# Adjacent-head pairs, stacked AV outputs and 64x64 diagonal transposes in a fused attention and bilinear-FFN kernel

## The chip, the cores and the metric

One Trainium2 chip, one of its cores. The metric is device time in microseconds (us) of one execution; lower is better. Each job below ran its kernels one after the other on the same chip, with runs of the kernel before between them. The record calls a run slow when it is over 1.5% above the fastest of the same kernel. The others are fast, and only they are compared: a ratio is the mean time of one kernel's fast runs over that of the other's fast runs of the same rounds. The medians and ranges quoted beside it are over all runs. They take in the slow ones, so the ratio is not quite that of the medians.

## The reference, cut to what matters

```python
# batch 8, heads 8, sequence 576, head 64; 8 global tokens; FFN 4608 tokens, 512 -> 1536 -> 512
mask = np.abs(pos[:, None] - pos[None, :]) <= 32
mask = mask | is_global[:, None] | is_global[None, :]
scores = np.where(mask, scale * np.matmul(q, k.transpose(0, 1, 3, 2)), -1e9)
attn = softmax(scores)                       # rows of global tokens see all keys
x = np.matmul(attn, v)                       # then heads side by side: (4608, 512)
out = ((x @ w_a) * (x @ w_b)) @ w_out
```

## The kernel before: the parts that the change and the argument touch

The kernel records every operation in a graph, and a list scheduler with fixed constants puts each engine's instructions into one static order. Attention of one batch is interleaved with the FFN of earlier ones. A "unit" is two heads over half of the sequence.

```python
# prologue: 14 warm-up matmuls of 512 columns, bound to PSUM bank 7
return e.matmul(psum[:, 7, :], onz[:, 0:2, :], HT[:, 0, 0:512], start=True, stop=True)

# q, k of the first two batches: one head's 64 rows at a time, transposed on PE,
# and the global tokens' columns by a chain of 9 one-hot matmuls (zeros and single ones, to pick columns)
for j in range(j0, j1):
    i = e.transpose(flat[:, 64 * j : 64 * j + 64], src[:, j, :], ident[xs, xs])
for j in range(9):
    i = e.matmul(gl, src[:, j, :], oh9[xs, j, x, :], start=(j == 0), stop=(j == 8), ...)

# rows of the global tokens: 8 plain transfers per tensor, the token from a register
src = (q, k, v)[t][:, :, bass.ds(regs[id(e), "tok"][gi], 1), :].rearrange("b h o d -> b (h o) d")
return e.dma_start((gathq, gathk, gathv)[t][gi::8, :, :], src)

# AV of a unit: V and ones side by side, 128 columns, one PSUM bank for each head
i = e.matmul(ops[:, hh, 0:OC]..., vb[sl][0:kk, c, hh, x : x + 2, :], eb[es][0:kk, hh, ...]...)
# then log, exp(-) and multiply on 64 partitions x 576; scatter of the 8 global tokens:
eng = ("DVE", "ACT")[gi % 2]
# ... cut ...
```

The softmax here doesn't subtract the row's maximum and nothing guards it: scores larger than these inputs give would overflow.

## Time and profile before

| | before |
|---|---|
| median (first job) | 395.75 us, 4 runs of 395.44 to 398.04 |
| PE busy, share of the span | 94% |
| first FFN matmul | 34.4 us |
| from there to the third 512-token FFN group | 92.5 us, PE idle 10.8 of them |
| from there to the end | 265.5 us |

The third group's start is taken here as the start of the ACT copy that follows its first matmuls (126.9 us). The three stretches add up to the span, so a difference between two kernels can be put into one of them. The profile's lines and how to read them are in the prediction below. Timeline columns: start, length, engine, source line, operation, times; in brackets the idle time before and what ended it.

```profile
123.10 0.56 DVE L610 COPY xT<-xg 128x4 bf16 x4
123.56 0.52 ACT L609 ACTIVATE xT<-xg 128x4 bf16 x4
...
124.14 0.61 PE L940 MATMUL psum<-xT,wb 128*128 128x512 bf16 x1 [1.28 <-ACT xT L609]
```

The scatter of eight tokens is shared by DVE and ACT, four copies each, and PE's FFN waits 1.28 us for its end.

### The profile page before, as it was taken

What the parts mean: (1) busy time and instruction counts of PE and PEld (TensorE: products, weight loads), DVE (VectorE), ACT (ScalarE), POOL (GpSimd) and SP (SyncE); (2) the same over time, 40 slices, a digit from 0 to 9 for tenths busy, and PEclk for the clock granted to TensorE, in tenths of its full rate; (3) what the DMA queues carried; (4) which work ended last, traced back from release to release, by engine and by line L of the source; (5) the groups of instructions that cost most, each with busy time, mean ns of one, the idle gap of its engine ahead of it and who ended that gap; (6) DMA issues with size and microseconds to landing.
All of it is one profiled execution on the core that took longest, in us unless ns stands there. A gap on an engine that the chain in (4) does not pass through costs nothing.

```text
span 392.4 us, 6734 instructions
## 1 busy us (share of the span) xinstructions
PE 368.4 (94%) x2532; PEld 190.1 (48%) x2532; DVE 242.9 (62%) x478; ACT 242.8 (62%) x417; POOL 97.6 (25%) x163
## 2 busy tenths in 40 slices
PE   3898998978985999999999999999999999999996
PEld 0567886434442444444444444444444444444442
DVE  6875688577877675867786677666767632222220
ACT  1576788676886676677776777776767633323322
POOL 5992095033813410601430430201000000000000
PEclk9569999899995999999999999999999999999999
DMA  6999999689897087966597636300000000100012
GB/s 217 255 282 184 201 243 173 153 226 275 195 270 173 14 118 185 250 171 155 186 229 161 189 90 162 90 28 27 29 28 28 27 27 28 53 28 27 34 48 107
DMA packets 122735, 52.66 MB, mean 134 GB/s; under 512 B 105143, under 2 KB 112879, under 8 KB 122703
## 3 DMA queue, kind: packets, MB, share of 16 engines
q1 hardware_dynamic: 113871, 47.24, 47.3%
q0 software_dynamic: 8352, 4.92, 8.6%
q8 instruction: 20, 0.33, 0.3%
q10 hardware_dynamic: 480, 0.07, 0.1%
q14 instruction: 12, 0.10, 0.1%
HBM read 39.97 MB, written 9.44 MB: 126 GB/s over the span
## 4 chain that ended last, share of the span: by engine, by line
PE 89%; DVE 7%; issue 1%; ACT 1%; POOL 0%; DVEq 0%; ACTq 0%
PE psum L940 48%; PE psum L977 24%; PE psum L839 7%; PE psum L757 5%; PE psum L792 2%; PE psum L685 2%; PE psum L752 1%; DVE xT L857 1%; DVE eb L830 1%; DVE HT L953 1%; PE psum L688 1%; PE psum L586 1%; DVE xT L610 1%; DVE kT L488 0%; DVE gsb L868 0%
## 5 line engine op out<-in xcount | busy, mean ns | idle before, releaser
L940 PE MATMUL psum<-xT,wb 128*128 128x512 bf16 (+2 forms) x480 | 127.7, 360 | 3.9 <-DVE xT L610 2.7
L940 PE MATMUL psum<-xT,wa 128*128 128x512 bf16 (+2 forms) x480 | 129.7, 360 | 0.0
L953 DVE TENSOR_TENSOR HT<-psum,bc 128x512 bf16<-128x512 f32 (+1 forms) x114 | 75.5, 663 | 81.4 <-PE psum L940 75.2
L977 PE MATMUL psum<-wo,HT 128*128 128x512 bf16 x432 | 123.8, 384 | 0.0
L948 ACT ACTIVATE bc<-psum 128x512 f32<-128x512 f32 (+1 forms) x114 | 65.5, 574 | 58.5 <-PE psum L940 57.3
L857 DVE TENSOR_TENSOR xT<-psum,rec 64x576 bf16<-64x576 f32 x56 | 64.3, 1148 | 12.9 <-ACT rec L854 12.0
L827 ACT ACTIVATE eb<-psum 128x960 bf16<-128x960 f32 x56 | 54.2, 969 | 22.1 <-PE psum L757 21.1
L940 PEld LDWEIGHTS psum<-xT,wb 128*128 128x128 bf16 x480 | 44.7, 98 | 46.7 <-ACT eb L827 2.9
L940 PEld LDWEIGHTS psum<-xT,wa 128*128 128x128 bf16 x480 | 45.5, 98 | 43.0 <-issue 0.9
L977 PEld LDWEIGHTS psum<-wo,HT 128*128 128x128 bf16 x432 | 40.0, 98 | 44.9 <-issue 3.8
L830 DVE TENSOR_TENSOR eb<-eb,mask 128x960 bf16<-128x960 bf16 x56 | 40.2, 718 | 20.8 <-ACT eb L827 20.1
L848 ACT ACTIVATE rec<-psum 64x576 f32<-64x576 f32 x56 | 36.0, 644 | 15.6 <-PE psum L839 15.0
L854 ACT ACTIVATE rec<-rec 64x576 f32<-64x576 f32 x56 | 37.9, 677 | 0.9
L984 ACT ACTIVATE ost<-psum 128x512 f32<-128x512 f32 x36 | 21.5, 597 | 26.9 <-PE psum L977 26.7
L839 PE MATMUL psum<-eb,vb 125*128 125x170 bf16 (+1 forms) x336 | 34.8, 244 | 2.6 <-DVE eb L830 2.6
L839 PEld LDWEIGHTS psum<-eb,vb 125*128 125x128 bf16 x336 | 29.2, 102 | 15.6 <-DVE eb L830 4.2
L757 PE MATMUL psum<-qT,kT 64*128 64x210 bf16 (+4 forms) x384 | 25.6, 241 | 5.3 <-DVE xT L857 4.6
L610 POOL CAST vb<-vs 128x640 bf16<-128x640 f32 (+2 forms) x26 | 17.6, 703 | 42.8 <-PE psum L839 42.8
L757 PEld LDWEIGHTS psum<-qT,kT 64*128 64x128 bf16 x384 | 11.8, 95 | 31.6 <-issue 13.4
L735 POOL COPY qT<-qgT 128x128 bf16<-128x128 bf16 x12 | 3.8, 322 | 89.2 <-PE psum L757 88.2
L637 POOL CAST kb<-ks 128x640 bf16<-128x640 f32 x24 | 17.9, 786 | 1.0 <-DMA ks<-in_k_dram 1.0
L850 DVE TENSOR_REDUCE gst<-psum 128x16 f32<-128x64 f32 x56 | 12.3, 219 | 8.2 <-ACT rec L848 7.5
(110 smaller groups left out, 232.0 us busy)
## 6 DMA issues: line engine op xcount, KB each, us to landing
vs<-in_v_dram SPq DMA_DIRECT2D x39, 256.0 KB, 3.9
out_dram<-ost SPq DMA_DIRECT2D x36, 256.0 KB, 2.0
qf<-in_q_dram SPq DMA_DIRECT2D x7, 1152.0 KB, 7.9
ks<-in_k_dram SPq DMA_DIRECT2D x30, 256.0 KB, 3.7
wb<-in_moe_w_b_dram POOLq DMA_DIRECT2D x6, 256.0 KB, 14.3
wa<-in_moe_w_a_dram POOLq DMA_DIRECT2D x6, 256.0 KB, 15.8
wo<-in_moe_w_out_dram POOLq DMA_DIRECT2D x6, 256.0 KB, 8.1
ks<-in_k_dram SPq DMA_DIRECT2D x2, 576.0 KB, 8.2
```

Of the source, the lines that this page charges most:

```text
L610: return e.tensor_copy(dst, src)
L757: i = e.matmul(psum[:, ob + hh, s0 : s0 + 10 * w].rearrange("p (j w) -> p j w", j=10), kT[rs][rw, 2 * c + x, :], qT[rs][rw, :, 64 * x + pa ...
L827: G.add("ACT", act_time(2 * SC), lambda e: e.activation(eb[es][:, :, :], sps[:, :, 0:SC], AF.Exp, scale=0.125), X=skeys, W=[("eb", es)], p ...
L830: G.add("DVE", dve_time(2 * SC, 2) + 0.06, lambda e: e.tensor_tensor(eb[es][:, :, :], eb[es][:, :, :], mask[:, r, :].unsqueeze(1).broadcas ...
L839: i = e.matmul(ops[:, hh, 0:OC].rearrange("p (j w) -> p j w", j=10)[:, :, pa - 32 * r : pb - 32 * r], vb[sl][0:kk, c, hh, x : x + 2, :], e ...
L848: G.add("ACT", act_time(576), lambda e: e.activation(rec[es][ro, :, :], ops[so, :, 0:288], AF.Ln), R=okeys, W=[("rec", es)], prio=prio + 1.2)
L854: G.add("ACT", act_time(576, False), lambda e: e.activation(rec[es][ro, :, :], rec[es][ro, :, :], AF.Exp, scale=-1.0), X=[("rec", es)], pr ...
L857: G.add("DVE", 1.12, lambda e: e.tensor_tensor(xT[ro, 2 * h : 2 * h + 2, t0 : t0 + 288].rearrange("p m (w j) -> p m w j", j=9), ops[ro, :, ...
L940: i = e.matmul(psum[:, bn, n * (f - fc) : n * (f - fc) + n], w[:, kc, 128 * f : 128 * f + 128], xT[:, kc, cols], start=(kc == 0), stop=(kc ...
L948: G.add("ACT", act_time(n * nf), lambda e: e.activation(bc[bi][:, 0 : n * nf], psum[:, bk, 0 : n * nf], AF.Copy), X=[("bank", bk)], W=[("b ...
L953: G.add("DVE", dve_time(n * nf), lambda e: e.tensor_tensor(HT[:, fc : fc + nf, hcol], psum[:, ak, 0 : n * nf].rearrange("p (f n) -> p f n" ...
L977: i = e.matmul(psum[:, ok, :], HT[:, fc, 512 * hs + 128 * tt : 512 * hs + 128 * tt + 128], wo[:, fc, :], start=(fc == 0), stop=(fc == NFC ...
```

## The change

Its intent: two neighbouring heads share a PSUM tile, V's product in one bank and the sums in another, so that log, exponential and multiply work on all 128 partitions; q and k are loaded on 128 partitions and transposed by diagonal 64x64 tiles; small warm-up matmuls fill PE's gaps until bank 7 is used. Inside the same diff: indirect gathers on POOL replace the register transfers, the scatter moves to ACT (batches 0, 1) and POOL (2 to 7), and all schedule constants are new.

```diff
 # transposes and one-hots, now twice as many, each on a 64x64 tile
-for j in range(j0, j1):
-    i = e.transpose(flat[:, 64 * j : 64 * j + 64], src[:, j, :], ident[xs, xs])
+for j in range(j0, j1):
+    for y, ys in halves:
+        i = e.transpose(flat[ys, 64 * j : 64 * j + 64], src[ys, j, :], ident[ys, ys])
 # ... one-hot chains likewise ...
 # AV
-i = e.matmul(ops[:, hh, 0:OC]..., vb[sl][0:kk, c, hh, x : x + 2, :], eb...)
+for n in range(2):
+    for x in range(2):
+        lh = ones[0:kk, 0:D] if n else vb[sl][0:kk, c, 2 * m + x, :]
+        i = e.matmul(acc[64 * x : 64 * x + 64, n, :]..., lh, eb[es][0:kk, x, ...]...)
 # global rows
-return e.dma_start((gathq, gathk, gathv)[t][gi::8, :, :], src)          # 8 per tensor
+e.indirect_dma_start(grow[t][:, D * n : D * n + D], None, src,
+                     bass.IndirectOffsetOnAxis(gidx[:, 0:1]..., 0), ...)  # POOL, 4 per tensor
 # scatter of global tokens
-eng = ("DVE", "ACT")[gi % 2]
+rk = ("regs", "ACT" if b == 1 else "POOL")
 # warm-up: up to 150 matmuls of 256 columns, where PE has nothing else
-for n in range(14): G.add("PE", 0.43, fn, ..., span=(4.0 + 0.45 * n, 12.0))
+for n in range(NFILL): G.add("PE", 0.15, fn, ..., span=(1.5, FILL), lat=0.0)
 # ... loads, casts, more than 20 constants: cut ...
```

## The prediction

> **What bounds the kernel now.** I read the page's busy table first, then the slices, then the busy time by stretch, then who waited for whom on PE, then single stretches of the timeline.
>
> ```profile
> PE 368.4 (94%) x2532; PEld 190.1 (48%) x2532; DVE 242.9 (62%) x478; ACT 242.8 (62%) x417; POOL 97.6 (25%) x163
> ...
> PE   3898998978985999999999999999999999999996
> ...
> PEclk9569999899995999999999999999999999999999
> ```
>
> PE is the bound: 94% busy, the others 62% or less. So the end is the sum of PE's work, its idle time and what it loses at a lower granted clock. The slices put idle and lost clock into the first third; from slice 14 on PE is full.
>
> ```profile
> 10.80:18.25 7.45, 7.40 (x113) 4.76 (x113) 6.16 (x14) 4.17 (x13) 7.45 (x14) 0.50 1.08 219
> ...
> 34.40:66.50 32.10, 32.10 (x423) 26.55 (x421) 23.18 (x59) 24.80 (x56) 17.69 (x25) 1.00 1.22 210
> 66.50:74.00 7.50, 5.37 (x34) 2.47 (x33) 5.68 (x13) 4.91 (x10) 0.61 (x1) 0.77 1.09 214
> 74.00:86.00 12.00, 11.48 (x78) 5.35 (x75) 7.21 (x13) 8.02 (x12) 1.14 (x4) 1.00 0.52 133
> 86.00:115.20 29.20, 26.52 (x180) 13.04 (x181) 23.56 (x38) 22.70 (x38) 14.16 (x20) 1.00 0.99 247
> 115.20:128.50 13.30, 7.81 (x46) 3.93 (x45) 8.89 (x20) 8.70 (x16) 3.96 (x7) 0.62 0.72 186
> 128.50:315.00 186.50, 185.50 (x1162) 89.38 (x1162) 131.65 (x229) 134.24 (x210) 35.19 (x54) 1.00 0.46 114
> ```
>
> Columns: stretch, its length, busy us of PE, weight load, DVE, ACT, POOL, granted clock, DMA share, GB/s. From 34.4 to 66.5 and after 128.5 PE is full at clock 1.00; only less PE work can help there. What can be won lies elsewhere: a late start (first transposes at 10.8 us), 15.3 us at half clock, and 66.5 to 128.5, where PE is busy 51.2 us of 62.0 (10.8 idle) and loses about 1.7 us (7.5 x 0.23) and 5.1 us (13.3 x 0.38) to the clock.
>
> ```profile
> PE psum L685 <- DVE kb L610: 5.4, 1, 5.4
> PE psum L757 <- DVE xT L857: 4.6, 3, 1.8
> PE psum L940 <- DVE xT L610: 2.7, 1, 2.7
> ```
>
> PE's waits, in us. Scores (L757) wait for the DVE multiply that frees their bank (L857), FFN (L940) for the scatter of the global tokens.
>
> ```profile
> L857 DVE TENSOR_TENSOR xT<-psum,rec 64x576 bf16<-64x576 f32 x56 | 64.3, 1148 | 12.9 <-ACT rec L854 12.0
> L848 ACT ACTIVATE rec<-psum 64x576 f32<-64x576 f32 x56 | 36.0, 644 | 15.6 <-PE psum L839 15.0
> L800 ACT ACTIVATE rec<-psum 128x288 f32<-128x288 f32 x8 | 3.3, 411 | 5.2 <-PE psum L792 5.2
> L810 DVE TENSOR_TENSOR xT<-psum,rec 128x288 bf16<-128x288 f32 x4 | 2.5, 646 | 0.4 <-ACT rec L806 0.2
> ```
>
> The kernel holds both layouts: 56 units do logarithm, exponential and multiply on 64 partitions x 576, the first batch on 128 x 288. The same amount of data costs 0.41 (logarithm) and 0.65 us (multiply) there against 0.64 and 1.15; the exponential's rows of the same view, L806 and L854, give 0.44 against 0.68.
>
> [...]clock 0.50 for 15.3 us after a gap from 5.5 to 10.8 us, and again near 71 and 118 us after waits. [...]from 10.8 to 18.25 us PE is busy 7.40 of 7.45 us, mostly with transposes, and stays at 0.50. [...]
>
> ```profile
> 219.27 0.60 PE L977 MATMUL psum<-wo,HT 128*128 128x512 bf16 x2
> 219.80 0.39 PE L757 MATMUL psum<-qT,kT 64*128 64x110 bf16 x6
> 220.12 0.60 PE L977 MATMUL psum<-wo,HT 128*128 128x512 bf16 x2
> ```
>
> Two FFN matmuls stream 0.43 us, to 219.70 (a matmul of 512 columns takes 0.2165 us in the full stretches); scores begin 0.10 later. Their three pairs of 110, 210 and 160 columns would stream 0.20 us if the two row tiles run together, to 220.00; FFN resumes 0.12 later. So pairs do run together, and each change of shape costs about 0.10 us.
>
> **The change part by part.**
>
> Stacked AV (attention weights times V; a unit is two heads over half of the sequence). A unit now issues 12 matmuls into 64-column tiles, with V and with ones, two heads side by side, in place of 6 matmuls of 128 columns (56 units) or of 24 for two units (first batch). Streaming in pairs is 960 columns, 0.40 us as before (an AV block between FFN matmuls now takes 0.44), but AV enters and leaves another shape. The static order of PE's instructions has 144 changes of shape before and 233 after: 89 x 0.10 = **+8.9 us** of PE time. In the first batch 24 matmuls took 1.94 and 1.77 us at full clock for two units; 2 x 0.6 replaces them: 8 units x 0.33 = **-2.6 us**, part of it before FFN starts and counted there.
> Beside it the 56 units lose 56 x (1.15 - 0.65) = 28 us of DVE and 56 x (0.23 + 0.24) = 26 us of ACT. Neither engine is the bound, so nothing of that is gained directly; but each unit's chain from scores to free bank gets about 1.0 us shorter, and that chain makes the waits of 66.5 to 128.5.
>
> Diagonal transposes. The count doubles, 144 to 288 transposes and as many one-hot matmuls, each on a 64x64 tile, in pairs. If the pairs run together, as the scores' do, nothing changes; I allow **+1 us**.
>
> Start. DVE's register load (the 1.85 us of "issue" at 7.19 us in the chain of waits), two memsets (0.66 us) and the eight small gathers on ACT (8.8 to 12.3 us, with the mask's squares right behind) go away; indirect gathers on POOL come instead. First keys land about 8 us (issue at 0.94, 7.1 to landing), so the first transposes can start near 9.6: -1.2 us. The mask for the first scores was ready at 17.6 us, and those scores ran at 18.25; with ACT free they can run near 14.5.
>
> Warm-up. 45 matmuls of 256 columns, not bound to bank 7, 38 of them ahead of the first transposes: some 16 at half clock (0.21 us each, twice half of 0.2165) and 22 at full, ending near 8.2 us, so the gap is under 2 us[...]. But few fill the transposes, so I expect a return to half clock around 12 to 20 us rather than none, and about half of the cold excess won (about 2.5 us). Together: FFN starts near 28 us, not 34.4: **-6.4 us**. DMA is near saturation over the first 40 us (share 1.08 to 1.36 in the stretches), and the second batch's q and k must land for transposes that come at 42 us now; I give back **+1.5 us** there.
>
> Middle. Idle and lost clock of 66.5 to 128.5 is 10.8 + 6.8 = 17.6 us. With a chain of some 5 us made 1.0 us shorter, less queueing on DVE and ACT, and output matmuls placed over the scatter (28 after the second batch's last AV, 16 before), I take nearly nine tenths to go, since nothing but attention's pace makes these waits: **-15.5 us**.[...]
>
> Sum: -6.4 + 1.5 - 15.5 + 8.9 + 1 = -10.5; a further -1 for the first batch's AV after FFN's start, and -1 because about a tenth of the added changes of shape lies before FFN's start, inside its estimate: -12.5. From 395.9 that is **383 us**.
>
> **The rivals.** (a) AV's weight loads become the bound[...]. The scores' loads in row tiles overlap (95 ns each, six of them in a block of 0.32 us), and loads hide behind FFN now (98 ns in 0.2165 us). If column tiles load one after another, a unit takes about 0.25 us more, 64 units +16 us, and the time is about 399. (b) The expected gain is hidden: PE merely waits for DMA or the POOL scatter instead, the prologue gains 3 us in place of 6.4, and the changes of shape eat the rest: 390 to 394. For it speaks the DMA share above 1 until 66 us; against it POOL's 25%. (c) Everything in the first 128 us is won, clock and idle alike, and pairs keep shapes together: 371 to 374.
>
> **Range and chances.** Middle 383; eight in ten from 371 to 394: (c) sets the lower end, (b) the upper; (a) is the tail beyond. Faster by over 2% is below 388: 0.74. Within 2%: 0.22. Slower by over 2%, above 404, needs (a) and a poor prologue: 0.04.
>
> **What would show it.** AV blocks near 0.60 us in the timeline with both column tiles starting together (right), or 0.85 and weight loads in a row (rival a). Logarithm, exponential and multiply at 0.41, 0.44 and 0.65 us x56. First transposes near 9.6 us, first FFN near 28 us, a granted clock above 0.50 in part of 10 to 26 us. PE idle below 5 us between FFN's start and the third 512-token group's, and PE full from there on, each such stretch some 2% longer for the same FFN matmuls. The prediction is wrong if PE's waits keep their size under other names, if the clock stays at half through the prologue, or if AV costs 0.8 us or more.

Not shown: that the 6.8 us of lost clock in the middle come back with the waits, that the clock stays up from the warm-up to the first transposes, and that warm-up matmuls among the transposes win about 2.5 us at half clock. Rival (a)'s 0.25 us for each unit, and its 0.85 for an AV block, are suppositions, worked out from no trace number. Half and full clock are the 0.50 and 1.00 of the profile's clock column.

## The result, and the profile after

The changed kernel took **413.79 us** (413.26 to 415.26, 4 runs) against 395.75 (ratio 1.045, 95% interval 1.040 to 1.050): slower by 4.5%, where 383 was predicted.

First the page's busy line and slices of the changed kernel.

```profile
PE 381.4 (92%) x3145; PEld 193.5 (47%) x3185; DVE 202.7 (49%) x411; ACT 212.9 (52%) x402; POOL 104.5 (25%) x179
...
PE   5695979979997799999999999999999999999996
...
PEclk9756788989999699999999999999999999999999
```

DVE and ACT lost 40 and 30 us of work, as planned, and PE, the bound, gained at least 13 us (40 of its matmul records, all after 80 us, are missing from this trace: 3145 matmuls against 3185 weight loads). The clock row still has its dips. Where the time went, by stretch (length, busy us of PE, weight load, DVE, ACT, POOL, then the granted clock): first the kernel before, then the changed one.

```profile
10.80:34.40 23.60, 22.18 (x270) 15.01 (x271) 17.88 (x46) 15.28 (x37) 18.49 (x31) 0.68 1.19 248
34.40:126.90 92.50, 81.67 (x749) 50.64 (x747) 68.52 (x142) 67.88 (x127) 37.56 (x55) 0.94 1.00 212
126.90:392.40 265.50, 261.38 (x1512) 123.53 (x1510) 149.51 (x258) 158.32 (x253) 35.19 (x54) 0.99 0.35 93
```

```profile
11.60:43.80 32.20, 24.35 (x416) 15.23 (x417) 14.47 (x36) 15.57 (x36) 23.43 (x30) 0.60 1.26 220
43.80:138.90 95.10, 84.18 (x968) 51.36 (x974) 58.20 (x122) 59.15 (x129) 26.45 (x39) 0.91 0.87 168
138.90:412.40 273.50, 267.11 (x1727) 122.56 (x1758) 123.49 (x219) 135.98 (x235) 46.66 (x84) 1.00 0.42 98
```

FFN starts 9.4 us later, the middle is 2.6 us longer with the same idle time of PE (95.10 - 84.18 = 10.9 against 92.50 - 81.67 = 10.8), and the rest is 8.0 us longer: together the 20.0 us between the two spans. The unit's operations are as predicted; the logarithm's row (0.410 us, 64 times) stands for them:

```profile
L829 ACT ACTIVATE rec<-psum 128x288 f32<-128x288 f32 x64 | 26.2, 410 | 53.1 <-PE psum L820 49.7
```

So the costs were read rightly, and what was to be won did not come. The late start is odd. Here is the timeline of the changed kernel where its first transposes should run one behind the other:

```profile
13.03 0.23 PE L702 MATMUL psum<-ident,kb 64*64 64x64 bf16 x3
13.77 0.26 PE L702 MATMUL psum<-ident,kb 64*64 64x64 bf16 x4 [0.51 <-issue]
13.83 0.94 POOL L568 DMA_INDIRECT grow<-in_v_dram,gidx  x1 [0.30 <-issue]
...
15.07 0.95 POOL L568 DMA_INDIRECT grow<-in_v_dram,gidx  x1 [0.30 <-issue]
15.26 0.29 PE L706 MATMUL psum<-oh,kb 64*64 64x8 bf16 x5 [0.50 <-issue]
...
16.86 0.20 DVE L628 CAST kT<-psum 128x40 bf16<-128x40 f32 x1 [3.79 <-remote]
```

PE issues four or five matmuls, rests half a us and goes on, waiting for nothing that the profile shows ("issue"). The semaphore update (the signal by which one engine tells others that its result is there) of its one-hot chain that ended at 13.16 us reached the other engines at 16.83: DVE's cast waited 3.79 us for it. In the trace's semaphore records, updates of PE, ACT and DVE came 1.3 to 4.3 us late at 13, 29, 32 and 36 to 38 us, none late after 40 us, and in the kernel before none at all.

Two theories. **T1**: PE runs out of instructions. The changed kernel has 6355 recorded PE instructions instead of 5102, about half of the surplus ahead of 62 us (doubled transposes and one-hots, and warm-up), and their fetches (the trace's queue of kind "instruction", 25 packets of 16 KB against 20) queue behind loads that keep the DMA share above 1. Both traces have one such packet for some 255 recorded PE instructions (5102 / 20, 6355 / 25), which fits the blocks of 256 of which the expectations below speak; where the blocks end is read at the third job. **T2**: POOL's indirect gathers, which lie in just these stretches (10.97 to 16.02 and 28.3 to 38.2 us), hold up PE's issue and the other engines' semaphore updates.

### The profile page after: what moved, and what is told of

The parts are those of the page before. It is cut to its first block, busy times and chain, and to the rows that moved or that the text cites. A ratio compares the mean times of both kernels' runs of the same rounds, so it can differ in the third digit from the quotient of the medians.

```text
span 412.4 us, 7906 instructions
## 1 busy us (share of the span) xinstructions
PE 381.4 (92%) x3145; PEld 193.5 (47%) x3185; DVE 202.7 (49%) x411; ACT 212.9 (52%) x402; POOL 104.5 (25%) x179
## 4 chain that ended last, share of the span: by engine, by line
PE 89%; issue 4%; DMA 2%; ACT 2%; DVE 2%; POOL 1%; ACTq 0%; POOLq 0%
PE psum L909 47%; PE psum L946 23%; PE psum L820 8%; PE psum L776 5%; DMA gtok<-in_global_idx_dram 2%; PE psum L702 2%; PE psum L706 2%; PE psum L771 1%; ACT eb L804 1%; PE psum L604 0%; POOL xT L628 0%; ACT rec L829 0%; DVE eb L808 0%; POOL vb L628 0%; DVE xT L841 0%
## 5 line engine op out<-in xcount | busy, mean ns | idle before, releaser
L909 PE MATMUL psum<-xT,wb 128*128 128x512 bf16 (+2 forms) x475 | 115.9, 365 | 2.8 <-POOL kT L758 2.5
L909 PE MATMUL psum<-xT,wa 128*128 128x512 bf16 (+2 forms) x457 | 112.9, 362 | 2.1 <-issue 1.3
L946 PE MATMUL psum<-wo,HT 128*128 128x512 bf16 x420 | 100.8, 382 | 1.9 <-issue 1.1
L804 ACT ACTIVATE eb<-psum 128x960 bf16<-128x960 f32 x64 | 61.5, 967 | 13.3 <-PE psum L776 12.5
L909 PEld LDWEIGHTS psum<-xT,wb 128*128 128x128 bf16 x480 | 43.8, 99 | 47.4 <-issue 5.1
L829 ACT ACTIVATE rec<-psum 128x288 f32<-128x288 f32 x64 | 26.2, 410 | 53.1 <-PE psum L820 49.7
L841 DVE TENSOR_TENSOR xT<-psum,rec 128x288 bf16<-128x288 f32 (+2 forms) x68 | 41.6, 619 | 8.3 <-ACT rec L835 7.0
L820 PE MATMUL psum<-eb,vb 125*64 125x210 bf16 (+4 forms) x384 | 38.4, 257 | 1.8 <-DVE eb L808 0.9
L820 PE MATMUL psum<-eb,ones 125*64 125x210 bf16 (+4 forms) x384 | 36.8, 250 | 0.0
L820 PEld LDWEIGHTS psum<-eb,vb 125*64 125x64 bf16 (+1 forms) x384 | 21.9, 117 | 24.6 <-DVE HT L922 9.7
L831 DVE TENSOR_REDUCE gst<-psum 128x16 f32<-128x64 f32 x64 | 14.0, 219 | 32.7 <-ACT rec L829 29.3
L835 ACT ACTIVATE rec<-rec 128x288 f32<-128x288 f32 x64 | 27.9, 441 | 1.6 <-ACT rec L829 0.2
L628 POOL CAST vb<-vs 128x1280 bf16<-128x1280 f32 (+1 forms) x13 | 15.8, 1222 | 39.5 <-PE psum L820 29.3
```

The source lines that it names most:

```text
L804: G.add("ACT", act_time(2 * SC), lambda e: e.activation(eb[es][:, :, :], psum[:, ob : ob + 2, 0:SC], AF.Exp, scale=0.125), X=keys, W=[("eb ...
L820: i = e.matmul(acc[xs, n, :].rearrange("p (j w) -> p j w", j=10)[:, :, pa - 32 * r : pb - 32 * r], lh, eb[es][0:kk, x, s0 : s0 + 10 * w].r ...
L829: G.add("ACT", act_time(288), lambda e: e.activation(rc[:], acc[:, 1, 0:288], AF.Ln), R=keys[1:], W=[("rec", es)], prio=prio + d[3])
L835: G.add("ACT", act_time(288, False), lambda e: e.activation(rc[:], rc[:], AF.Exp, scale=-1.0), X=[("rec", es)], prio=prio + d[5])
L841: G.add("DVE", 0.06 + nw * 0.0185, lambda e, w0=w0, w1=w1, c0=c0, nw=nw: e.tensor_tensor(xT[:, kc, c0 : c0 + 9 * nw].rearrange("p (w j) -> ...
L909: i = e.matmul(psum[:, bn, n * (f - fc) : n * (f - fc) + n], w[:, kc, 128 * f : 128 * f + 128], xT[:, kc, cols], start=(kc == 0), stop=(kc ...
```

## The experiments

The edits are against the changed kernel, unless a line says otherwise. "Quick" and "slow" chips are explained at the third job.

**First job: one part undone at a time.**

```diff
-e.indirect_dma_start(grow[t][:, D * n : D * n + D], None, src, bass.IndirectOffsetOnAxis(gidx...), ...)
+e.dma_start(grow[t][:, D * n : D * n + D], bass.AP((q, k, v)[t].tensor, n * S * D, [[4 * S * D, 16], [D, NG], [1, D]]))
```

> The twelve indirect gathers on POOL become plain transfers of the same shape, from fixed rows (wrong result on purpose; the order of every engine is that of the changed kernel). Theory T2 (POOL's indirect gathers hold up PE's issue and its semaphore updates): the slow stretch of transposes at 13.3-16.8 us and the updates that came 2.6 to 3.7 us late go; the first FFN matmul comes at about 38 us instead of 43.8; time 407 to 410. Theory T1 (PE runs out of instructions because its fetches wait behind loads): the late stretches stay, the first FFN matmul within 1 us of 43.8, time 412 to 415.

404.23 us (402.59 to 405.67; before in this job 396.42), first FFN matmul at 34.4 us, no late update. By itself this looks like T2, though better than its 407 to 410; the other runs of the job spoil that.

```diff
-NFILL = 150
+NFILL = 0
```

> No warm-up matmuls at all (the other engines' order unchanged). T1: 45 matmuls and 45 weight loads fewer move the fetches by a third of a block and ease little; T2: no effect on the waits. Both: [...]the first FFN matmul stays within 1.5 us of 43.8 and the time within 411 to 416. If the warm-up did pay, it is 2 us or more slower.

405.17 us (404.41 to 405.46), first FFN matmul at 33.5 us.

```diff
-for j in range(9):            # one-hot chain per half
+for j in range(1):
```

> Each one-hot chain of 9 matmuls per half is cut to one (wrong values for the global tokens, on purpose): 256 matmuls and 256 weight loads fewer on PE before 60 us, the order of all else unchanged. T1: PE crosses one to two 256-instruction blocks fewer, so stalls of fetch come later or go: the stall of 2.85 us at 56.6 us and part of those at 13-37 us go, first FFN matmul at 38 to 40 us, time 405 to 409. T2: the waits beside the gathers stay; only the matmuls' own time on the path is saved, some 1 to 2 us: first FFN matmul at 42 to 43, time 411 to 413.

396.00 us (395.01 to 397.89), the time of the kernel before (ratio 1.000, 0.995 to 1.005); first FFN matmul at 32.7 us, and no stall at the second batch's transposes. About half of the 8 us against x1 is simply the work left out: a chain of nine one-hots pairs 18 matmuls in 0.28 us, one of one 2 in 0.03, and there are 16 such chains (an estimate of 4 us at full clock). The rest is about the size of x1's two stalls at block edges (0.7 and 4.0 us, read below). (The result passed as correct, within the tolerance, but is wrong for global tokens.)

```diff
-WT = -10.56; WS = 1.12        # when and how far apart FFN weights are issued
+WT = 6.0; WS = 2.67           # as in the kernel before
```

> The FFN weights are issued by the schedule constants of the kernel before (later and further apart) instead of the changed ones. T1 and the view that early weight transfers crowd the queues: fetches and first loads land sooner, the first FFN matmul comes 2 to 4 us earlier (40 to 42), time 409 to 412. T2: no gain; time 413 or worse, as weights may then come late (up to 418).

405.33 us (404.32 to 405.98), first FFN matmul at 32.1 us. Against x1 (404.23) nothing was gained: FFN began earlier and then waited 2.65 us for weights.

None of the eight ranges that the two theories had given for these four times was met; all four runs came in below them. Four unlike edits had each brought FFN's start back from 43.8 to 32-34 us, and none showed an update over 1 us late, though three of them keep the indirect gathers. Either everything cures it, or this chip did not have it. The control was missing.

**Second job: the control.**

> The changed kernel as it is, beside its own variants, because four unlike edits each took the first FFN matmul from 43.8 to 32-34 us. If the late stretches at 13-17 and 29-40 us (semaphore updates of PE and ACT 1.3 to 4.3 us late) belong to the kernel, its first FFN matmul is again at 43-44 us and its time 413 to 415. If they belong to a chip or an execution, its first FFN matmul comes at 33 to 36 us and the time is 403 to 406, as in the variants without warm-up or with later weights.

412.16 us (410.69 to 415.57; before 397.39), first FFN matmul at 44.0, late updates at 14 and from 29 to 37 us: as in the first result. On this chip every run had late updates.

> Both: no warm-up matmuls and one-hot chains of one matmul. T1 (fetch): up to the second batch's transposes PE meets no fetch stall of over 2 us, time 393 to 397, as with few one-hots alone (396.0); the warm-up itself worth nothing. If warm-up was a cost of its own (8.6 us when taken alone), 387 to 390.

400.87 us (397.45 to 405.30), with late updates at 13 to 16 us and from 30 to 39 us, so not to be compared with x3. It has no stall at a block edge before 60 us, as T1's branch said, but not that branch's time.

```diff
 # batches 2 to 7
+i = e.matmul(acc[:, x, :]..., vb[sl][0:kk, c, m, x : x + 2, :], eb[es][0:kk, x, ...]...)   # 128 columns
+# log on two halves of 64 partitions, multiply likewise
```

> Batches 2 to 7 take the kernel before's product of values and ones (128 columns, no column tiles), with two Ln and two multiplications per unit in place of one. Column tiles and changes of tile shape cost 0.23 us on each of 48 units: third FFN group's start to the end 264 to 266 us instead of 275, time 10 to 12 us below the changed kernel of the same job. If DVE and ACT (some 30 and 20 us more work) bound that stretch instead, it gains less than 4 us.

412.60 us (410.65 to 413.77), no gain as a whole. Two things in it, the middle and third group to the end:

```profile
36.10:145.30 109.20, 89.11 (x946) 54.10 (x952) 64.33 (x134) 67.94 (x150) 33.37 (x48) 0.86 0.92 174
145.30:409.40 264.10, 258.68 (x1479) 123.32 (x1506) 146.38 (x265) 155.44 (x274) 36.91 (x78) 1.00 0.39 95
```

The end is 8.6 us shorter than in y1 of the same job (272.7), as the price of column tiles and shape changes would have it (0.18 us for each of 48 units). But the middle is 14.5 us longer than y1's 94.7, with 20.1 us of PE idle against 11.3. Part of that is where the cut falls: y3's FFN starts 7.9 us earlier (36.1 against 44.0), so that late updates of 36 to 43 us lie inside its middle, and its third group starts only 6.6 us later than y1's (145.3 against 138.7). Its fetch stalls are longer too (5.4 us against 3.0). But PE's waits for DVE there are 10.4 us against 2.9, so the lighter work of DVE and ACT is worth something in this order; how much was not separated.

```diff
-NFILL = 150                                  +NFILL = 0
-GPRIO = 3.37                                 +GPRIO = -100005      # q, k gathers right after v's
 # second batch: global columns copied from the gathered rows, no one-hot matmuls
```

> No warm-up; the second batch's global columns come from the gathered rows, as those of batches 2 to 7 do, not from one-hot matmuls (288 PE instructions fewer before 60 us, right result); the gathers of q and k are issued right after those of v. T1: the 4 us fetch stall at the second batch's transposes goes with the half clock that it causes: 397 to 400, against 405.2 for no warm-up alone. T2: gathers now lie in the first batch's transposes: late semaphore updates of over 1 us at 16 to 26 us, and 404 or more.

408.57 us (407.89 to 409.23): T2's branch of the expectation. The late updates moved with the gathers, up to 10 us late between 13 and 28 us, and the transposes of that stretch crawl between the gathers, as here:

```profile
17.54 0.94 POOL L569 DMA_INDIRECT grow<-in_q_dram,gidx  x1 [0.31 <-issue]
18.23 0.34 PE L703 MATMUL psum<-ident,qb 64*64 64x64 bf16 x5 [1.12 <-issue]
```

First FFN matmul only at 45.4 us. Yet PE has no "issue" gap over 0.6 us left at the second batch's transposes, where y1 has one of 2.2, and the middle is 89.3 us against y1's 94.7: there T1's branch was right. (About 2 us of PE work went with the one-hots, eight chains of 0.28 us; the same holds for w3, w4, h2 and k2 below.)

**Third job: the same question, on a chip without late updates.**

> The changed kernel as it is once more, as the control for the plain gathers on this chip: if its late semaphore updates of PE and ACT are there (over 1 us, at 13-17 and 29-40 us), first FFN matmul at 43-45 us and 411 to 415 us; if not, 34 us and 402 to 406, and then the job with plain gathers alone has told nothing.

403.40 us (402.54 to 405.89; before 397.10), first FFN matmul at 34.4. The changed kernel has two speeds, by chip: 412 to 414 where updates come late ("slow" chips), 403 where they do not ("quick"). On a quick chip it is 1.8% slower than the kernel before (ratio 1.018, 1.011 to 1.025). The kernel before has medians of 394.7 to 397.4 on both sorts. The first and the fourth job fell on one chip, quick both times, the third on another quick one, and the slow jobs (y and z, i, k) on three others.

> Plain transfers in place of the indirect gathers (wrong result on purpose, order unchanged), now beside the changed kernel itself. T2: no semaphore update over 0.5 us late, first FFN matmul at 34 to 35 us, 402 to 405, on a chip where the changed kernel shows them. If they are late here too, the gathers are not the cause: 411 to 415.

404.72 us (403.37 to 404.88), first FFN matmul at 35.9 us: on a quick chip plain gathers change nothing, so x1 had told nothing about T2. (It is x1's kernel; the start differs by 1.5 us from one job to the other.)

Undisturbed by late updates, w1 shows T1 alone. Its timeline at the second batch's transposes:

```profile
46.15 0.29 PE L702 MATMUL psum<-ident,kb 64*64 64x64 bf16 x8
...
49.84 0.34 PE L702 MATMUL psum<-ident,kb 64*64 64x64 bf16 x10 [3.40 <-issue]
```

PE stops in the middle of a run of equal transposes. Numbered through all PE instructions in the trace, the stop lies behind the 1473rd. I then numbered every gap of over 0.6 us before 100 us in all runs that ends with "issue" and no wait: the first result has one behind instruction 1473; w1 and w2 behind 449, 705 and 1473; x1, x2, x4 and h1 (below) behind 449 and 1473, x2 also behind 1217; y1, y3 and k1 (below) behind 1473 and 1729; i1 (below) behind 449 and 1729. All are 193 + a multiple of 256, and elsewhere such gaps are found only in the crawl of slow chips, before 45 us: these are the edges of the instruction blocks. In w1 PE ran the block up to 1473 in 2.97 us (43.28 to 46.25); the packet with the next one was moved at 47.32 to 48.31, and PE went on at 49.84, 6.6 us after it had entered the block. The first result has the same: a block entered at 53.46 and done in 2.97 us, the packet at 57.07 to 57.96, PE on at 59.47. x4 ran this block in 2.3 us and then stood 4.3. The kernel before never needs less than 5.1 us for a block before 100 us, and has no such gap. In x3 the block that ends nearest to the second batch's transposes takes 5.2 us, and PE has no such gap at all: T1 is shown, with its cure. A short block alone does not make the stall: in i1 (below) one of 2.97 us is followed by a gap of only 0.6 us. When the packet comes differs: in the kernel before the first five begin 2.2 to 2.9 us after PE has entered a block, in the first result the first seven 1.3 to 4.6 us after. Beside the stall itself comes a lower clock: 0.50 from 50 to 55 us in x2, behind a stall of 4.1, and 0.58 in h1 (below), behind one of 4.05, where in the same stretch it is 1.00 in x3 and in the kernel before.

```profile
51.00:60.00 9.00, 9.00 (x131) 6.54 (x128) 3.67 (x9) 3.96 (x8) 4.46 (x6) 0.58 1.07 211
```

9 us at a mean clock of 0.58 lose about 9 x 0.42 = 3.8 us (an estimate), beside the 4.05 of the stall. A caution for other clock figures: the runs without warm-up have no clock record before 22 to 39 us and the profile counts that as 1.00, though 18 one-hots took 0.48 us at 12.85 us in h2 against 0.28 at full clock in w1. The mean clocks of such runs are not to be compared with the others'.

Next, a right result without either cause:

```diff
-e.indirect_dma_start(...)                     # 4 per tensor
+e.dma_start(grow[t][gi::8, :]..., src of bass.ds(regs[id(e), "tok"][gi], 1))   # POOL, by register
 # with NFILL = 0 and the second batch's globals from gathered rows, as in z1
```

> Right result: gathers by register, as the kernel before had them, on POOL; the second batch's global columns from the gathered rows (no one-hots there); no warm-up. T1 and T2 together: no late updates, no fetch stall over 1.5 us at the second batch's transposes, first FFN matmul at 33 to 36 us; 394 to 399. If POOL's longer issue of 32 gathers holds up weights or masks, first FFN matmul at 38 or later and 401 to 405.

404.42 us (400.76 to 405.62): no late update, no stall at a block edge, and yet nothing was gained, as FFN's matmuls waited 6.1 us for weights. That these came late because they now stood behind 32 register gathers on POOL is read from the order; h2 below, where some gathers are put behind them, fits. The second branch of the expectation had the result, though not its mechanism: FFN started at 31.9 us and ran dry later.

```diff
 # w3, and batches 4 to 7 take the 128-column product of y3
```

> The same, and batches 4 to 7 take the kernel before's 128-column product of values and ones: 32 units x 0.23 us = 7 us less PE time in the steady stretch, where DVE and ACT have room (some 45% busy): 387 to 392, under the kernel before's 396. If the extra Ln and multiplications cost what the tiles gave, within 2 us of the run without it.

396.39 us (393.50 to 397.72; before 397.10): a tie, and 8 us under w3 as expected, though above the 387 to 392 named, as w3 itself was late. Third group to the end, first w3, then w4:

```profile
129.40:402.50 273.10, 266.32 (x1716) 121.98 (x1748) 123.51 (x218) 135.84 (x234) 46.30 (x84) 1.00 0.41 96
```

```profile
129.80:396.00 266.20, 260.40 (x1527) 123.57 (x1554) 142.47 (x257) 154.64 (x271) 41.60 (x80) 1.00 0.42 99
```

6.9 us less for 32 units, 0.22 us each. The extra log and multiply cost nothing there, as DVE and ACT are 54 and 58% busy.

**Fourth job and the next run: T2 with its control inside.** v's four gathers plain, those of q and k indirect; the order of instructions unchanged, the result wrong.

> The four gathers of v plain (wrong result on purpose), the eight of q and k still indirect, order unchanged: one kernel as its own control. T2 on a chip of the slow sort: no update over 0.5 us late before 25 us, updates of PE and ACT over 1 us late between 28 and 40 us, beside the gathers of q and k; first FFN matmul at 37 to 41 us. If the late updates stand before 18 us too, the gathers are not their cause. On a chip of the quick sort: none at all, 34 us, 402 to 405, and nothing told.

404.24 us (403.84 to 405.54): a quick chip, no late update, nothing told.

> As for the first kernel with half of the gathers plain: on a chip of the slow sort T2 expects no update over 0.5 us late before 25 us and updates of PE and ACT over 1 us late between 28 and 40 us, first FFN matmul at 37 to 41 us; late updates before 18 us too would clear the gathers. On a chip of the quick sort: none, 34 us.

One single run, its state unknown, 407.63 us (before 393.36): a slow chip at last. No update was late before 25 us, and the first transposes ran without the crawl; between 28 and 36 us updates of PE came up to 3.2 and those of ACT up to 9.4 us late; first FFN matmul at 40.3 us, inside the range that T2 gave.

```profile
34.88 0.95 POOL L568 DMA_INDIRECT grow<-in_k_dram,gidx  x1 [0.30 <-issue]
35.62 0.41 ACT L829 ACTIVATE rec<-psum 128x288 f32<-128x288 f32 x1 [3.82 <-PE psum L776]
...
36.06 0.22 DVE L831 TENSOR_REDUCE gst<-psum 128x16 f32<-128x64 f32 x1 [3.55 <-issue]
```

ACT waited 3.82 us for a product that had been done 2.2 us before, at 33.4, up to the end of the last gather (34.88 + 0.95 = 35.83). With z1 this shows T2, though i1 is a single run: the late updates go where the indirect gathers go, and v's plain gathers on the same POOL queue brought none. Why only some chips do it stays open.

```diff
 # w4, with the register gathers of the first batch's v ahead of the rest (8 transfers), q and k after four weights
+VREST = -5; GPRIO = -5
 # ... two cost constants of the scheduler for AV, changed too: cut ...
```

> Register gathers with those of the first batch's v ahead, the second batch's globals from gathered rows, no warm-up, stacked values and sums for batches 0 to 3 and the 128-column product for batches 4 to 7. No late updates on any chip under T2. First FFN matmul at 31 to 34 us, no fetch stall over 1.5 us, third FFN group to the end 265 us: 389 to 394, at least 1% under the kernel before. If the first AV still waits for v's gather, or FFN weights come late, 395 to 398.

390.0 us median (389.01 to 396.53; before 394.70), ratio 0.986 (0.979 to 0.993): faster than both kernels, result right. A gain of 1.4% over the kernel before is under the 2% that the record counts as clear, but its interval leaves out 1. About 2 us of it can be the one-hot chains left out, which the kernel before still runs. Which of its edits made the gain over w4 was not separated.

**Last job, a slow chip: the wait before the third group.**

```diff
-rk = ("regs", "ACT" if b == 1 else "POOL")    # scatter of the global tokens
+rk = ("regs", "ACT")
```

> The changed kernel with the scatter of batches 2 to 7 on ACT in place of POOL; the order is the same up to that scatter. Theory: the eight copies take 1.0 to 1.1 us and PE's wait before the third FFN group falls from 2.47 to 1.3-1.6 us. Rival: that wait stays within 0.3 us of 2.47. The whole: within 2 us of the changed kernel, 402 to 404 on a quick chip, 411 to 414 on a slow one.

412.79 us (411.62 to 416.49), the whole unchanged within some 2 us: the changed kernel itself did not run in this job, only in others. The changed kernel first, then this run, at the same place:

```profile
134.59 0.19 DVE L866 TENSOR_TENSOR xg<-gsb,grc 128x32 bf16<-128x32 f32 x1
134.96 1.98 POOL L628 COPY xT<-xg 128x4 bf16 x8 [1.82 <-DVE xg L866]
...
137.00 0.13 PEld L909 LDWEIGHTS psum<-xT,wb 128*128 128x128 bf16 x2 [2.43 <-POOL xT L628]
137.40 1.06 PE L909 MATMUL psum<-xT,wb 128*128 128x512 bf16 x2 [2.47 <-POOL kT L758]
```

```profile
131.28 0.19 DVE L866 TENSOR_TENSOR xg<-gsb,grc 128x32 bf16<-128x32 f32 x1
131.60 0.97 ACT L627 ACTIVATE xT<-xg 128x4 bf16 x8 [0.66 <-DVE xg L866]
...
132.63 0.61 PE L909 MATMUL psum<-xT,wb 128*128 128x512 bf16 x1 [4.32 <-ACT xT L627]
```

In the changed kernel the first FFN matmul's record is missing: its weights are loaded at 137.00, and the matmul at 137.40 is the next one. So from the end of xg (134.78) to FFN it is 2.22 us with POOL, 1.16 with ACT, and 1.18 in the kernel before (xg ends at 122.96). The scatter on POOL is in PE's path and costs about 1.1 us. The figure of the wait itself did not fall to 1.3-1.6 as expected: the new order put scores behind FFN, so that the wait for the whole tail shows as one of 4.32 us. That half of the expectation missed, though the third group came earlier, at 135.6 us against 138.9 (middle 92.7 us).

> The mended version with the same edit, on whatever chip: no late semaphore updates on either sort, first FFN matmul 31 to 33 us, 388 to 392, at least 1% under the kernel before of the same job. If ACT, 8 x 0.13 us per batch more, delays exponentials, 392 to 394.

389.28 us (389.05 to 389.46; before 395.78), ratio 0.985 (0.979 to 0.991), on a slow chip, with no late update. Without indirect gathers the version keeps its speed on both sorts.

| run | us | before, same job | chip |
|---|---|---|---|
| changed, first result | 413.8 | 395.8 | slow |
| y1 changed again | 412.2 | 397.4 | slow |
| w1 changed, third time | 403.4 | 397.1 | quick |
| x3 few one-hots | 396.0 | 396.4 | quick |
| w4 mended start, 128-column AV late | 396.4 | 397.1 | quick |
| h2 mended | 390.0 | 394.7 | quick |
| k2 mended, scatter on ACT | 389.3 | 395.8 | slow |

## Why the prediction was wrong, point by point

**"FFN starts near 28 us ... -6.4 us": this step failed.** It came at 43.8 us (+9.4) on slow chips and at 34.4 us (0.0) on quick ones. On slow chips the indirect gathers, counted in the step only as work that replaces small transfers, held up issue and semaphores for some 10 us. On quick chips three things ate the gain. The warm-up ran from 4.9 us, where a DVE memset let it go, to 10.7 on the slow chip and to 11.4 to 12.1 on the quick ones (w1, x1), not to 8.2. (In the first result 14 of its 38 matmuls ahead of the first transposes came 0.21 us apart, up to 7.9 us, and the others 0.11 apart, near the forecast's 16 and 22; half clock was back from 14.7 to 31.8 us, not 12 to 20.) The first transposes came at 11.6 in the first result and in w1, not 9.6, since DVE, in its static order, first waited 2.7 us for the token numbers of the gathers, 8.6 us under way (in x1 the warm-up held them to 12.1). And PE stood 1.8 us at a block edge at 16.1 us in w1. Warm-up bought nothing: on one chip, FFN started at 33.5 us without it (x2) and at 34.4 with it (x1).

**"Middle ... -15.5 us": this step failed most.** On a quick chip the middle took 93.6 us against 92.5, and PE was idle 11.3 us against 10.8. Here is w1's:

```profile
34.40:128.00 93.60, 82.31 (x966) 50.25 (x974) 58.61 (x122) 59.09 (x130) 30.21 (x44) 0.93 1.01 184
```

The step took the waits as attention's pace and a shorter chain as their cure. In this it was half right: PE's waits on attention's DVE operations (for xT and eb) fell from 6.2 to 2.8 us. But other waits took their place, so that the sum stayed: a fetch stall of 3.4 us that was not there before, and 1.6 us behind POOL's copies (0.5 before), of them about 1.1 for the scatter ahead of the third group (k1). This is the prediction's own sign of being wrong, waits that "keep their size under other names". The clock fell as before, 0.93 against 0.94, first behind the fetch stall (50 to 57 us) and again before the third group (122 to 129). The step's 17.6 us also counted some time twice: the 5.1 us lost to the clock was taken over 13.3 us, of which PE was busy only 7.8. The stall alone does not explain the miss: without it the middle was still 89.9 (x3), 91.9 (h2) and 89.3 us (z1), 2 to 4 less, where about 77 was forecast. The other 12 or more were not separated; the new order and constants are part of it, and that stays open.

**"144 changes of shape before and 233 after: ... +8.9 us": right in kind and size.** Of the 89 added changes 72 lie behind the third group's start, where the kernel lost 8.0 us: 0.11 us each. w4 has 62 fewer than w3 there and took 6.9 us back, 0.11 each again. An AV block took 0.57 us between FFN matmuls at 41.1 us in w1, near the 0.60 forecast.

**"I allow +1 us" for the diagonal transposes: this term failed in kind.** The pairs do run together (18 in 0.29 us, where 9 took 0.27 before). The price of doubling lay in the count of instructions: a block of 256 lasted 3 us (2.97 in w1) instead of 5.1 or more, and PE stood 3.4 us behind it. With 256 fewer one-hot matmuls the whole was 8 us quicker (x3 against x1, same chip), about half of it by these stalls and half by the work left out.

**The rivals.** (a), weight loads as AV's bound, asked for 0.25 us per unit on top of the changes of shape; all together it was 0.22, of which the changes of shape alone make 0.19 (62 x 0.10 / 32), so (a) is refuted. (A 64-column load took 117 ns on average in the changed kernel, a 128-column one of FFN 98.) (b) named the right kind (DMA and the POOL scatter in place of what was won) and missed the size, since neither instruction fetch nor late semaphores was in it. (c) is refuted: nothing of the first 128 us was won. "DMA is near saturation" was read, but only for data. In us, on the slow chip: start 9.4 + middle 2.6 + rest 8.0 = 20.0; on the quick one (w1): 0.0 + 1.1 + 7.3 = 8.4.

## What to carry to other kernels

Count instructions for each us, not only busy time: where PE met many tiny matmuls while DMA was full (share 1.42 around the stall in h1), blocks of 256 instructions done in 2.3 to 3.0 us (x4, w1, the first result) were followed by stalls of 2.9 to 4.3 us, and the clock was lower behind them (0.58 over 9 us in h1). The kernel before, whose shortest block before 100 us took 5.1 us, had none. Keep indirect gathers out of stretches in which other engines hand work on by semaphores: beside them updates of PE, ACT and DVE came 1 to 10 us late in four of the seven jobs (first result, y and z, i, k), and not at all or under 1 us late in the others, on other chips. So run a control of the same kernel in every job: the changed kernel took 412 to 414 us on one sort of chip and 403 on the other, its predecessor 394.7 to 397.4 on both. The work taken off DVE and ACT (40 and 30 us), which were not the bound, paid only where a wait of the bound ended with it (PE's waits on attention's DVE operations, 6.2 to 2.8 us in w1); look whether the same diff puts another engine at the end of that wait (POOL's scatter, 1.1 us, k1).
